# FFN1 of a gated-loop kernel wholly in three one-pass products, FFN2 plain, gates in two parts with five slots

## The chip, the cores and the metric

The kernel runs on one core of one Trainium2 chip. The metric is device time in microseconds (us). The profiler takes one execution apart: PE is TensorE (matmul), PEld its weight loads, DVE VectorE, ACT ScalarE, POOL GpSimd, SP SyncE, which here only issues DMAs.

## What is computed

A linear recurrence with complex decay per head (4 batches, 8 heads, 768 steps, head size 48), whose output goes as x (3072 x 384) into a feed-forward part:

```python
mag = np.sqrt(a_re * a_re + a_im * a_im)
scale = np.minimum(mag, 0.999) / (mag + 1e-06)       # a_n = a * scale
for t in range(S):
    S_re, S_im = ar*S_re - ai*S_im + outer(k[t], v[t]), ar*S_im + ai*S_re
    y[t] = q[t] @ S_re
x = y.transpose(0, 2, 1, 3).reshape(B * S, H * D)
out = (((x @ w1) * (x @ w2)) @ w3) @ w_out            # d_ff = 1024
```

Inputs are f32; the weights come as 64-bit floats and are rounded to f32 on the chip.

## The kernel before

**Units.** A unit is half a batch: 384 steps (TT) of all 8 heads, so there are eight (NU), in order. A unit has three stages.

- *Gates* (`gates`, passes over 128 x 1152 on ACT and DVE): logarithms and exponentials of the magnitude, arctangent, running product and running sum, sine and cosine, and from them q and k times cosine and sine (line 788 R = k*cos, 791 A = q*cos, 795 k*sin, 799 q*sin). Then DMAs ("move") lay them out by head in QL and KL. QL and KL exist once, so a unit's moves wait for the end of the unit before. The gates of u+1 begin with `gate_head` (Ln and Exp of re); the im rows of u+1 are loaded when lines 788 and 791 of u are done, as they take re's buffer.
- *Attention pieces* (`pieces`): transposes of R and k into KT ("tr"), states ("kv"), scores ("sc", with a masked copy on DVE), outputs ("y"). From unit 2 (THREE) on, "y" also makes three rounded forms of x: x0 on ACT, x1 on DVE, x2 on POOL.
- *FFN*: FFN1 makes a = x w1 and b = x w2 for eight blocks of 128 columns (j) and ab = a*b; FFN2 multiplies ab by w3o = w3 w_out (made once at the start), three tiles of 128 rows a unit.

**Products.** A plain product is three f32 matmuls (128 x 128 by 384 columns); the profile has two instructions for each. A *three-product* form splits weight and x into a coarse and a fine fp32r part, each multiplied in one pass: "hb" does coarse x coarse and fine x fine (six instructions), ACT rescales the PSUM bank in place (line 945), "db" adds the third product (three instructions) to the same bank, and DVE multiplies it into ab (line 929). Before, this holds for six of the 16 products of a unit, from unit 2 on: b for j < 6 (J3). The split weights are made once (`split_ops`: line 967 on ACT, 970 and 972 on DVE), in place of the whole ones, three of them (NB).

**FFN2** from unit 1 on takes tiles in pairs and multiplies 2 x 2 blocks with seven products instead of eight (`out_sums`, `out_pair`, line 1049: four matmuls of 192 columns each, sums on DVE). Every third tile is kept (`keep`) for a pair with the next unit's.

**Order.** The PE's order is a list: `unit(u, rest, ahead)` begins with AHEAD[u] items of the FFN of u-1, then mixes the rest of it with the pieces of u. The gates' steps, the splits and the checks are generators that yield (engine, cost, name, what it waits for); `run` walks the list, keeps a clock for each engine, and puts a step into its engine's queue where it `fits` before the next request of the list plus a slack (SLACK, LATE, EARLY). All engines run their queues in order. PSUM has four banks for the FFN (`ps_m`), two for tr, kv and y (`ps_v`).

**Memory.** A, R, q and k of a unit live in slots, six of them; the table SLOTS says which. The k and q rows of a unit are loaded in the middle of its gates, V rows (`load_v`) beside its predecessor's last state; the V tile with heads side by side (`turn_v`, 14 DMAs) is loaded after the predecessor's last y.

**Checks.** POOL looks through gates and weights for values that the fast path does not cover (`check_weights`); the last part of w3 is squared on POOL and tested on ACT (lines 1198, 1200). If one is found, a slow general kernel runs after all.

The lines that load k and q, that put the plain products ahead of the three-product ones, and that begin a unit's list:

```python
            if u > 2 and u not in LATER:      # gates(u), after the first logarithms
                load_qkv(u)
            ab = [[x for y in ab[J3:] for x in y] + [y.pop(1) for y in ab[:J3]]] + ab[:J3]   # ffn(u)
        seq = [("begin", u)] + rest[:ahead]   # unit(u)
```

Of the kernel before, what the change touches and what calls it, by code (L numbers as in the profile page):

```python
# [378 lines left out]
def kernel(  # L379
# [61 lines left out]
    J3 = NB * WB // P  # L441
    LATER = ()
# [29 lines left out]
    SLOTS = [dict(A=0, R=1, q=2, k=3), dict(A=4, R=5, q=0, k=2)]  # L472
# [69 lines left out]
    def take_qk(u):  # L542
        g = g_t.setdefault(u, {})
        g["q"] = slot(u, "q", "q")[:, :, 0:TT]
        g["k"] = slot(u, "k", "k")
# [7 lines left out]
    def load_qkv(u, key=None):  # L553
        b, h = divmod(u, 2)
        if "q" not in g_t.get(u, {}):
            take_qk(u)
        g = g_t[u]
        load_rows(g["k"], kt, u, key=key)
        load_rows(g["q"], qt, u)
        landed(("q", u), (), *(() if u in SPLIT else (2, 2.4)))  # L560
# [30 lines left out]
    def gate_head(u):  # L591

        g = g_t[u]
        g["A"], g["R"] = slot(u, "A", "gA")[:, :, 0:TT], slot(u, "R", "gR")
        yield "ACT", 2.45, "a1", (("re", u),)
        chain(nc.scalar.preload_act_table_set("natural_log_exp_and_others"))
        chain(nc.scalar.activation(out=g["A"], in_=g["re"], func=AF.Ln))
        yield "ACT", PASS, "r1", ("a1",)
        chain(nc.scalar.activation(out=g["R"][:, :, 0:TT], in_=g["A"], func=AF.Exp, scale=-1.0))

    def gates(u, split):
# [3 lines left out]
        if "A" not in g:  # L605
            g["A"], g["R"] = slot(u, "A", "gA")[:, :, 0:TT], slot(u, "R", "gR")
        A, R = g["A"], g["R"]
        Z = one.tile([P, KD, TT], FP, tag="gZ", name="gZ")
        re, im = g["re"], g["im"]
        r = R[:, :, 0:TT]  # L610
# [6 lines left out]

        if u < 2:
# [3 lines left out]
            for s in parts:  # L622
                act(out=A[:, s], in_=re[:, s], func=AF.Ln)
                yield "ACT", PASS, "r1", ("a1",)
                act(out=r[:, s], in_=A[:, s], func=AF.Exp, scale=-1.0)
# [7 lines left out]
        for i, s in enumerate(parts):  # L633
            yield "DVE", WIDE, "im", ("r1", ("im", u))
            tt(out=im[:, s], in0=im[:, s], in1=r[:, s], op=OP.mult)  # L635
# [11 lines left out]
        def operands():  # L647
            if u > 2 and u not in LATER:
                load_qkv(u)
            elif "q" not in g:  # L650
                take_qk(u)
            return g["q"], g["k"], g["k"][:, :, 0:TT]
        early = u > 1
        if early:
            q, K2, k = operands()
# [11 lines left out]
        for s in parts:  # L667
            yield "DVE", 1.0, "min", ("a2",)
            ts(out=A[:, s], in0=A[:, s], scalar1=0.999, scalar2=None, op0=OP.min)
            for f in range(s.start, s.stop):  # L670
                yield "DVE", SCAN, "mag", ("min", "z3")
                nc.vector.tensor_tensor_scan(out=A[:, f], data0=A[:, f], data1=Z[:, f], initial=1.0,  # L672
                                             op0=OP.mult, op1=OP.mult)
                if u > 1 and f < 2:
                    yield "ACT", 1.45, "low", ("im",)
                    check_gates(u, re, r, f)
        yield None

        for s in parts:
# [5 lines left out]
        if not early:  # L685
            q, K2, k = operands()

# [6 lines left out]
        def scaled(s):  # L694
            yield "DVE", WIDE, "k", ("r2", ("q", u))
            tt(out=k[:, s], in0=k[:, s], in1=r[:, s], op=OP.mult)
            if not early:
                yield "DVE", WIDE, "q", ("mag", ("q", u))
                tt(out=q[:, s], in0=q[:, s], in1=A[:, s], op=OP.mult)

        def ends():
            yield "ACT", 0.6, "ends", ("k",)
            for X in (R[:, :, TT], K2[:, :, TT], st_dec[:, u]):
# [5 lines left out]
        if u > 0:  # L709
            if early:  # L710
                yield "DVE", WIDE, "q", ("mag", ("q", u))
                tt(out=q, in0=q, in1=A, op=OP.mult)
# [23 lines left out]
        if u + 1 < NU:  # L736
            load_gates(u + 1, ("re",), ("ang",))
        yield None
# [23 lines left out]
        QL = one.tile([2 * D, H, TT], FP, tag="QL", name="QL")  # L762
        L_t[u] = QL, KL, R, K2
# [19 lines left out]
        if 0 < u < NU - 1:  # L783
            ops = gate_head(u + 1)
            g_t[u + 1]["head"] = [next(ops), ops]
            others.append(g_t[u + 1]["head"])
# [23 lines left out]
    def turn(u, c, x):  # L810
# [7 lines left out]
        with tc.high_priority():  # L818
            nc.scalar.copy(out=KT_t[u, c][:, :, :, x].rearrange("p h d f -> p f d h"),  # L819
                           in_=tp.rearrange("p f (d h) -> p f d h", h=H))  # L820

# [23 lines left out]
    def outputs(u, c):  # L845
# [3 lines left out]
        if c == 0:  # L849
            xT_t[u] = one.tile([P, KD, TT], FP, tag="xT", name="xT")  # L850
            if u >= THREE and NB:
# [15 lines left out]
        with tc.high_priority():  # L867
            if u in x_t:
                x = [t[:, :, w] for t in x_t[u]]
                nc.scalar.activation(out=x[0], in_=y, func=AF.Copy, scale=TOP / BITS)  # L870
# [5 lines left out]
            last["y", u, c] = nc.scalar.copy(out=xT_t[u][:, :, w], in_=y)  # L876
# [5 lines left out]
    def state(u, c):  # L882
# [19 lines left out]
        if 1 < u + 1 < NU and u + 1 not in LATER and c == UC - 1 - u % 2:  # L902
            load_v(u + 1)

    def ffn_ab(u, j):
# [32 lines left out]
        def heads():  # L938
            if u == THREE:
                while split_t[0] <= n and split_next():  # L940
                    pass
            got.append(bank())
            product(got[0], [(w3_h[n][:, :, w], x_t[u][0]), (w3_l[n][:, 0, :, w], x_t[u][1])])
            with tc.high_priority():
                nc.scalar.activation(out=got[0], in_=got[0], func=AF.Copy, scale=1.0 + 1.0 / BITS)  # L945

        def diffs():
            product(got[0], [(w3_l[n][:, 1, :, w], x_t[u][2])], False)
            times(got[0])

        if u >= THREE and j < J3:
            return [("hb", heads), ("ab1", first), ("db", diffs)]
# [8 lines left out]
    def split_ops():  # L961
        for n in range(NB):
            tag = f"w{n - 1}1" if n else "x0"
            yield "ACT", 0.85, ("head", n), (("tail", n - 1),) if n else ()
            pool = w12 if n else late[0]
            h = w3_h[n] = pool.tile([P, KD, WB], FR, tag=tag, name="wh", **({} if n else dict(padded_shape=[P, KD, TT])))
            nc.scalar.activation(out=h, in_=w_t[n][1], func=AF.Copy, scale=TOP * BITS)
            L = w3_l[n] = late[0].tile([P, 2, KD, WB], FR, tag=f"low{n}", name="low")
            yield "DVE", 1.0, ("tail", n), (("head", n),)
            nc.vector.scalar_tensor_tensor(out=L[:, 0], in0=w_t[n][1], scalar=BITS, in1=h, op0=OP.mult, op1=OP.subtract)  # L970
            yield "DVE", 1.0, ("diff", n), (("tail", n),)
            nc.vector.scalar_tensor_tensor(out=L[:, 1], in0=h, scalar=1.0 / BITS, in1=L[:, 0], op0=OP.mult, op1=OP.subtract)
            if n == NB - 1:
                yield "ACT", 0.85, ("head", 0), (("tail", n),)
                h = w12.tile([P, KD, WB], FR, tag=f"w{n}1", name="wh")
                nc.scalar.activation(out=h, in_=w3_h[0], func=AF.Copy)
                w3_h[0] = h
# [11 lines left out]
    KH, DH = KF // 2, DM // 2  # L989
    s_t = {}  # L990

    def out_weights():
        T = s_t["T"] = late[0].tile([P, 3, KH, DH], FP, tag="T", name="To")
        B = [[w3o[:, i * KH:(i + 1) * KH, j * DH:(j + 1) * DH] for j in range(2)] for i in range(2)]
        s_t["B"] = B[0][0], B[1][0], B[1][1], T[:, 2], T[:, 0], T[:, 1], B[0][1]
        for out, x, y in ((T[:, 0], B[0][1], B[0][0]), (T[:, 1], B[1][1], T[:, 0]), (T[:, 2], B[1][0], T[:, 1])):
            yield "DVE", 0.96, "out", ()
            nc.vector.tensor_tensor(out=out, in0=x, in1=y, op=OP.subtract)

    def last_weights():  # L1000
        B = s_t["B"]
        if len(B) == 7:
            nc.vector.tensor_tensor(out=B[6], in0=B[2], in1=B[6], op=OP.subtract)
            s_t["B"] = *B, None

    def keep(u):
        s_t["kept"] = late[0].tile([P, KF, P], FP, tag="kept", name="kept")
        nc.scalar.copy(out=s_t["kept"], in_=ab_t[u][:, :, 2 * P:3 * P])

    def out_sums(tiles):  # L1010
        S = s_t["S"] = late[0].tile([P, 3, KH, P], FP, tag="S", name="So")
        A = [[(s_t["kept"] if kept else ab_t[u][:, :, t * P:(t + 1) * P])[:, i * KH:(i + 1) * KH] for i in range(2)]
             for u, t, kept in tiles]
        s_t["sums"] = []
        with tc.high_priority():
            for i, (out, x, y, op) in enumerate(((S[:, 0], A[1][0], A[1][1], OP.add), (S[:, 1], S[:, 0], A[0][0], OP.subtract),
                                  (A[1][0], A[0][0], A[1][0], OP.subtract), (S[:, 2], A[0][1], S[:, 1], OP.subtract))):
                if i > 1:
                    s_t["sums"].append((out, x, y))
                else:  # L1020
                    nc.vector.tensor_tensor(out=out, in0=x, in1=y, op=op)
        s_t["A"] = A[0][0], A[0][1], S[:, 2], A[1][1], S[:, 0], S[:, 1], A[1][0]

    def out_pair(tiles):
        m, U, o = {}, {}, {}

        def add(out, x, y):
            nc.vector.tensor_tensor(out=out, in0=x, in1=y, op=OP.add)

        def done(t, half):  # L1030
# [712 lines left out]
```

## Time and profile before

| | |
|---|---|
| median of 3 runs | 540.72 us (537.26 to 541.58) |
| profiled execution | 539.31 us, span 537.5 us |
| PE busy | 505.5 us (94%) |
| DVE, ACT, POOL busy | 385.0, 314.9, 304.9 us |
| mean granted TensorE clock | 0.985 |

Busy time of an engine is the union of its instructions; matmuls overlap at their ends. "x552" counts instructions. A wait row names the instruction that waited, what released it, the total, the number of times and the longest. A row of the chain is start, length and what; its pieces follow one another without overlap. A row of windows is a stretch, its length, and busy time of each engine with the number of instructions, then the granted clock and the DMA share.

### The profile page before, as it was taken

How to read it: one execution, taken by the hardware profiler on the slowest of the kernel's cores; microseconds unless marked ns; L12 is line 12 of the kernel's file. 1: busy time of each engine (PE TensorE's matmuls, PEld its weight loads, DVE VectorE, ACT ScalarE, POOL GpSimd, SP SyncE). 2: the span in 40 equal slices, each digit the busy share in tenths (PEclk: the TensorE clock that was granted, in tenths of full speed). 3: DMA queues.
4: the chain of work that ended last, by engine and by line, in shares of the span. 5: the costliest groups of instructions: out<-in, count | busy, mean ns of one | idle time of the engine just before them, and what ended most of it. 6: DMA issues, size and time to landing. Idle time of an engine off the chain costs nothing.

```text
span 537.5 us, 13680 instructions
## 1 busy us (share of the span) xinstructions
PE 505.5 (94%) x5654; PEld 383.7 (71%) x5654; DVE 385.0 (72%) x581; ACT 314.9 (59%) x489; POOL 304.9 (57%) x343
## 2 busy tenths in 40 slices
PE   5689799998999999999998999999989999999994
PEld 2355575555756795888587985997679967995894
DVE  7999698867499888576857986688659882640171
ACT  6979866546566927646568426844777143258500
POOL 1000000028788989678967899669979898543000
PEclk9899899999999999999998999999999999999997
DMA  8999876694839736973598449955597247533001
GB/s 287 370 408 265 168 243 179 163 216 113 162 87 212 183 90 176 235 200 88 132 223 185 124 98 220 196 137 140 142 187 184 71 125 177 194 102 126 0 32 35
DMA packets 72456, 89.75 MB, mean 167 GB/s; under 512 B 30784, under 2 KB 62208, under 8 KB 71616
## 3 DMA queue, kind: packets, MB, share of 16 engines
q1 hardware_dynamic: 66464, 69.77, 51.5%
q0 software_dynamic: 5920, 19.01, 12.5%
q8 instruction: 46, 0.75, 0.6%
q14 instruction: 26, 0.21, 0.1%
HBM read 65.14 MB, written 4.72 MB: 130 GB/s over the span
## 4 chain that ended last, share of the span: by engine, by line
PE 67%; DVE 12%; ACT 8%; DMA 7%; issue 4%; SPq 1%; DVEq 0%; ACTq 0%
PE m L913 29%; PE p L1049 17%; PE y L866 7%; DMA im<-in_a_im_dram 5%; PE sc L831 5%; PE kv L891 2%; PE f L1339 2%; ACT gZ L614 2%; PE tp L817 2%; DVE gZ L732 2%; PE o L1087 1%; ACT KT L819 1%; ACT re L614 1%; DVE im L635 1%; DVE gA L672 1%
## 5 line engine op out<-in xcount | busy, mean ns | idle before, releaser
L913 PE MATMUL m<-xT,ws 128*128 128x384 f32 x552 | 180.0, 486 | 1.2 <-ACT xT L876 1.2
L913 PEld LDWEIGHTS m<-xT,ws 128*128 128x128 f32 x552 | 104.3, 190 | 71.9 <-ACT xT L876 1.7
L1227 POOL TENSOR_SCALAR look<-look 128x256 f32<-128x256 f32 (+1 forms) x64 | 77.9, 1218 | 5.6
L929 DVE TENSOR_TENSOR ab<-m,ab 128x384 f32<-128x384 f32 x64 | 35.1, 552 | 58.8 <-PE m L913 31.1
L925 ACT COPY ab<-m 128x384 f32<-128x384 f32 x64 | 30.1, 474 | 57.3 <-PE m L913 57.2
L1189 POOL TENSOR_TENSOR seen<-seen,look 128x256 bf16<-128x256 bf16 (+1 forms) x64 | 59.2, 925 | 5.2
L1173 POOL MEMSET seen<- 128x256 bf16 x1 | 0.3, 317 | 108.9 <-DVE ab L929 108.9
L913 PE MATMUL m<-x,low 128*128 128x384 f32 x216 | 47.8, 346 | 2.8 <-ACT m L945 2.7
L1224 POOL TENSOR_TENSOR look<-look 128x256 f32<-128x256 f32 (+1 forms) x52 | 38.7, 743 | 20.7 <-DMA look<-in_w_dram 12.9
L913 PEld LDWEIGHTS m<-x,low 128*128 128x128 f32 x216 | 37.9, 188 | 4.3 <-ACT m L945 4.2
L866 PE MATMUL y<-A,V 128*32 128x128 f32 x768 | 39.9, 272 | 0.4 <-issue 0.4
L870 ACT ACTIVATE x<-y 128x384 fp32r<-128x384 f32 x18 | 8.8, 491 | 51.8 <-PE y L866 51.8
L819 ACT COPY KT<-tp 128x384 f32<-128x384 f32 x40 | 34.7, 872 | 7.1 <-PE tp L817 6.9
L834 DVE COPY_PREDICATED A<-mask,sc 128x512 f32<-128x512 uint8 x48 | 32.6, 730 | 6.0 <-PE sc L831 6.0
L866 PE MATMUL y<-QL,T 96*32 96x128 f32 x640 | 35.5, 272 | 0.0
L866 PEld LDWEIGHTS y<-A,V 128*32 128x32 f32 x768 | 34.4, 110 | 0.9 <-issue 0.9
L1049 PE MATMUL p<-w3o,ab 128*128 128x192 f32 x192 | 35.0, 331 | 0.0
L831 PE MATMUL sc<-QL,KL 96*32 96x32 f32 (+3 forms) x1536 | 32.1, 235 | 1.5 <-DVE A L834 1.2
L1339 PE MATMUL f<-wo_s,w3s 128*128 128x384 f32 x96 | 33.4, 495 | 0.0
L1226 POOL TENSOR_SCALAR look<-look 128x192 f32<-128x192 f32 (+1 forms) x24 | 26.6, 1107 | 11.4 <-DMA look<-in_a_re_dram 10.0
L831 PEld LDWEIGHTS sc<-QL,KL 96*32 96x32 f32 x1536 | 28.4, 110 | 6.3 <-issue 3.4
L1049 PEld LDWEIGHTS p<-w3o,ab 128*128 128x128 f32 x192 | 31.8, 193 | 0.4 <-issue 0.2
(152 smaller groups left out, 1072.0 us busy)
## 6 DMA issues: line engine op xcount, KB each, us to landing
look<-in_w_dram POOLq DMA_DIRECT2D x36, 256.0 KB, 4.3
raw<-in_w_dram SPq DMA_DIRECT2D x6, 1024.0 KB, 9.9
looked<-in_w_dram POOLq DMA_DIRECT2D x10, 512.0 KB, 4.4
KL<-gR SPq DMA_DIRECT2D x24, 192.5 KB, 3.2
KL<-k SPq DMA_DIRECT2D x24, 192.5 KB, 6.9
vr<-in_v_dram SPq DMA_DIRECT2D x8, 576.0 KB, 6.4
QL<-gA SPq DMA_DIRECT2D x24, 192.0 KB, 7.4
QL<-q SPq DMA_DIRECT2D x24, 192.0 KB, 7.5
```

The costliest lines, as they stand in the source:

```text
L819: nc.scalar.copy(out=KT_t[u, c][:, :, :, x].rearrange("p h d f -> p f d h"), in_=tp.rearrange("p f (d h) -> p f d h", h=H))
L831: nc.tensor.matmul(out=sc[SB * g:SB * g + SB, j, s0:C], lhsT=KL[:, x * n + j, w][:, s0:s0 + SB], rhs=QL[:, x * n + j, w][:, s0:C], start=T ...
L834: last["sc", u, c, x] = nc.vector.copy_predicated(out=A[:, x * n:(x + 1) * n], data=sc, mask=mask)
L866: nc.tensor.matmul(out=o, lhsT=a, rhs=b, start=s0, stop=s1)
L913: nc.tensor.matmul(out=out, lhsT=a, rhs=b, start=start and i == 0, stop=i == len(terms) - 1, skip_group_check=not start)
L925: nc.scalar.copy(out=ab_t[u][:, j], in_=m)
L929: last["ab", u, j] = nc.vector.tensor_tensor(out=ab_t[u][:, j], in0=m, in1=ab_t[u][:, j], op=OP.mult)
L1049: nc.tensor.matmul(out=m[p], lhsT=a[:, f], rhs=b[:, f], start=(f == 0), stop=(f == KH - 1))
L1189: nc.gpsimd.tensor_tensor(out=seen[:, 0:n], in0=seen[:, 0:n], in1=x, op=OP.add)
L1224: tt(out=x, in0=x, in1=x, op=OP.mult)
L1227: ts(out=x, in0=x, scalar1=low, scalar2=None, op0=OP.is_ge)
L1339: nc.tensor.matmul(out=sums[j], lhsT=w3_t[f][:, j * P:(j + 1) * P], rhs=w3_t["wo"][:, f], start=(f == 0), stop=(f == KF - 1))
```

## The change

- **FFN1**: from unit 2 on every product, of w1 and of w2, is in three one-pass products. The tail of the w1 product ("da") is copied to ab by ACT, that of w2 ("db") multiplied by DVE. Heads run two ahead of tails (DEEP). Eight weight splits instead of three; all must be done before the first y of unit 2, since one uses x0's buffer for a time. x is no longer copied to xT from unit 2 on.
- **FFN2**: plain tiles; `out_weights`, `out_sums`, `out_pair`, `keep` go.
- **Gates** from unit 2 on (`gates_apart`): every pass in two parts, of 384 and 768 columns; five slots; the two range checks of re move into the head, ahead of its Ln; Exp of the head goes to re's buffer.
- **Loads**: k, q and V rows of u+1 are issued at the end of unit u, the first of them held behind the last y of u. For unit 2, k and q are issued at a transpose of unit 1.
- **Order**: `unit` shares the FFN out by planned PE time, not by count; AHEAD is in us. Slacks are wider. POOL's looks are held off 9 us before an x instead of 3. w3's late tests go from ACT to DVE. Two early weight loads are issued somewhat later.

```diff
-    AHEAD = [0, 3, 12, 15] + [8] * (NU - 4)
+    AHEAD = [0, 0, 23.0, 25.0] + [14.0] * (NU - 4)
-    PASS, WIDE, SCAN, LAND, SLACK, LATE, RING, NEAR, EARLY = 1.17, 1.48, 1.08, 1.8, 1.8, 2.4, 8, 4, 2
+    PASS, WIDE, SCAN, LAND, SLACK, LATE, RING, NEAR, EARLY = 1.17, 1.48, 1.08, 1.8, 2.6, 3.0, 8, 4, 2
-    THREE, NB = 2, 3
+    THREE, DEEP = 2, 2
-    HOLD, COSTS = 3.0, (4.9, 4.5, 6.8, 2.5)
+    HOLD, COSTS = 9.0, (4.9, 4.5, 6.8, 2.5)
-        SLOTS.append(dict(A=SLOTS[u - 2]["R"], R=SLOTS[u - 2]["k"], q=SLOTS[u - 1]["A"], k=SLOTS[u - 1]["q"]))
+        SLOTS.append(dict(A=SLOTS[u - 2]["k"], R=SLOTS[u - 1]["A"], q=SLOTS[u - 1]["q"], k=SLOTS[u - 1]["R"]))
+    def gates_apart(u, A, Z):
+        parts = [(0, slice(0, 1)), (1, slice(1, KD))]
...
+        for i, s in parts:
+            yield on("DVE", "im_", i, "r1", ("im", u))
+            tt(out=im[:, s], in0=im[:, s], in1=re[:, s], op=OP.mult)
...
+        for i, s in parts:
+            yield on("DVE", "kc_", i, ("cos_", i), ("k_", i))
+            tt(out=r[:, s], in0=k[:, s], in1=re[:, s], op=OP.mult)
+            move(KL, R, 0, i, s, "kc_")
...
+        if u + 1 < NU:
+            load_gates(u + 1, ("im",), (("kc_", 1), ("qc_", 1)))
...
+        def heads(m):
...
+            product(got[m], [(h[:, :, w], x_t[u][0]), (low[:, 0, :, w], x_t[u][1])])
+            with tc.high_priority():
+                nc.scalar.activation(out=got[m], in_=got[m], func=AF.Copy, scale=1.0 + 1.0 / BITS)
+        def diffs(m):
+            product(got[m], [(w3_l[n, m][:, 1, :, w], x_t[u][2])], False)
+            if m:
+                return times(got[1])
+            with tc.high_priority():
+                nc.scalar.copy(out=ab_t[u][:, j], in_=got[0])
+        if u >= THREE:
+            return [("hb", lambda: heads(0)), ("da", lambda: diffs(0)), ("hb", lambda: heads(1)), ("db", lambda: diffs(1))]
...
+    def ffn(u):
+        ab = [x for j in range(KF) for x in ffn_ab(u, j)]
+        if u >= THREE:
+            h, d = ab[0::2], ab[1::2]
+            ab = h[:DEEP] + [x for p in zip(h[DEEP:], d) for x in p] + d[-DEEP:]
+        return ab + [(("part", "half")[n], f) for t in range(UC) for n, f in enumerate(ffn_out(u, t, 2))]
...
             elif kind == "end":
...
+                if 0 < f < NU - 1:
+                    if f > 1:
+                        load_of(f + 1, "k", ("y", f))
+                        load_of(f + 1, "q")
                     load_v(f + 1)
```

More of the change, by code (lines that the diff above doesn't have):

```diff
@@ L593, in gate_head @@
         g = g_t[u]
-        g["A"], g["R"] = slot(u, "A", "gA")[:, :, 0:TT], slot(u, "R", "gR")
-        yield "ACT", 2.45, "a1", (("re", u),)
+        re = g["re"]
+        A = g["A"] = slot(u, "A", "gA")[:, :, 0:TT]
+        for f in range(2):
+            yield "ACT", 1.45, "low", (("re", u),)
+            check_gates(u, re, A, f)
+        if not g["go"]:
+            yield None
+        yield "ACT", 2.45, "a1", ("low",)
         chain(nc.scalar.preload_act_table_set("natural_log_exp_and_others"))
-        chain(nc.scalar.activation(out=g["A"], in_=g["re"], func=AF.Ln))
+        chain(nc.scalar.activation(out=A, in_=re, func=AF.Ln))
@@ L849, in outputs @@
         if c == 0:
-            xT_t[u] = one.tile([P, KD, TT], FP, tag="xT", name="xT")
-            if u >= THREE and NB:
+            if u < THREE:
+                xT_t[u] = (late[0].tile([P, KD, TT], FP, tag="x1", name="xT") if u else
+                           cv["early"].tile([P, KD, TT], FP, tag="xT", name="xT"))
+            else:
+                while u == THREE and split_next():
+                    pass
                 x_t[u] = [late[0].tile([P, KD, TT], FR, tag=f"x{i}", name=f"x{i}") for i in range(3)]
@@ L875, in outputs @@
                 later.append(rest)
-            last["y", u, c] = nc.scalar.copy(out=xT_t[u][:, :, w], in_=y)
+            else:
+                last["y", u] = nc.scalar.copy(out=xT_t[u][:, :, w], in_=y)
     Tb = [singles.tile([2 * D, H, 64], FP, name=f"T{i}") for i in range(3)]
@@ L961, in split_ops @@
     def split_ops():
[L962 to L977, printed above, removed]
+        which = [(n, m) for n in range(FF // WB) for m in (1, 0)]
@@ new lines, in split_ops @@
+        for i, (n, m) in enumerate(which):
+            yield "ACT", 0.85, ("head", i), (("tail", i - 1),) if i else ()
+            w = w_t[n][m]
+            if i:
+                h = w12.tile([P, KD, WB], FR, tag="w%d%d" % which[i - 1], name="wh")
+            else:
+                h = late[0].tile([P, KD, WB], FR, tag="x0", padded_shape=[P, KD, TT], name="wh")
+            w3_h[n, m] = h
+            nc.scalar.activation(out=h, in_=w, func=AF.Copy, scale=TOP * BITS)
+            L = w3_l[n, m] = late[0].tile([P, 2, KD, WB], FR, tag=f"low{n}{m}", name="low")
+            yield "DVE", 1.12, ("tail", i), (("head", i),)
+            nc.vector.scalar_tensor_tensor(out=L[:, 0], in0=w, scalar=BITS, in1=h, op0=OP.mult, op1=OP.subtract)
+            yield "DVE", 1.12, ("diff", i), (("tail", i),)
+            nc.vector.scalar_tensor_tensor(out=L[:, 1], in0=h, scalar=1.0 / BITS, in1=L[:, 0], op0=OP.mult, op1=OP.subtract)
+            if i == len(which) - 1:
+                yield "ACT", 0.85, ("head", 0), (("tail", i),)
+                h = w12.tile([P, KD, WB], FR, tag="w%d%d" % which[i], name="wh")
+                nc.scalar.activation(out=h, in_=w3_h[which[0]], func=AF.Copy)
+                w3_h[which[0]] = h
@@ L1000, in last_weights @@
[L1000 to L1022, printed above, removed]
@@ L1467, in start @@
     def start(op):
-        return max([clock[op[0]]] + [ready.get(x, 1e9 if type(x) is tuple and x[0] == 'q' else 0.0) for x in op[3]])
+        return max([clock[op[0]]] + [ready.get(x, 1e9 if type(x) is tuple and x[0] in ('q', 'k') else 0.0) for x in op[3]])
     def book(op):
```

413 lines of the change are left out of this document (228 added, 185 removed), and 5 rows, old and new, of the table TIMES.

## The prediction

> **What bounds the kernel now.** I read the page's head first, then the windows view cut at the ends of the units' last y, then the PE's waits.
>
> ```profile
> span 537.5 us, 13680 instructions
> ## 1 busy us (share of the span) xinstructions
> PE 505.5 (94%) x5654; PEld 383.7 (71%) x5654; DVE 385.0 (72%) x581; ACT 314.9 (59%) x489; POOL 304.9 (57%) x343
> ```
> ```profile
> sum 342.00, PE 336.45 PEld 267.64 DVE 254.40 ACT 193.39 POOL 276.72; mean PE 56.08 PEld 44.61 DVE 42.40 ACT 32.23 POOL 46.12
> ```
> ```profile
> PE m L913 <- ACT m L945: 2.7, 4, 0.8
> ```
>
> The sum row covers 140 to 482 us, six unit periods of 57 us on average: the PE is busy for 336.45 of 342 us. The other engines have room (DVE 254, ACT 193). So a microsecond less of matmul is a microsecond less of span, as long as nothing else becomes late; and all the PE ever waited for in FFN1 is 2.7 us, four times, for the scaling on ACT between the two halves of a three-product result (L945). There is little else to win: idle PE time in the middle is 5.5 us in all.
>
> **The change, part by part.** Rates come from the chain that ended last, where a piece starts when the one before ends, so pieces do not overlap.
>
> ```profile
> 166.34 1.94 PE m L913 x6
> ...
> 174.10 5.18 PE o L1087 x16
> ...
> 226.93 1.58 PE m L913 x9
> ...
> 511.25 6.50 PE p L1049 x40
> ...
> 517.88 11.91 PE p L1049 x72
> ```
>
> *FFN1.* A plain product (three f32 matmuls, two instructions each) takes 1.94 us, the same product as nine one-pass matmuls 1.58. In units 2 to 7 there are 16 products a unit, 96 in all; 36 are in three products already (six a unit). The change converts 60: 60 x 0.36 = **-21.6 us**.
>
> The Trainium skill, "TensorE: Matmul & The Clock Gate", section "Back-to-back issue gap", gives N/2.4 + 2.5 ns for a warm matmul, 162.5 ns for 384 columns; by it, as an estimate, nine would take 1.46 us, the term would be -28.8 and the time 526.5. The trace has 1.58 / 9 = 176 ns; it disagrees, the row decides, and the rule gets no chance of its own.
>
> *FFN2.* The seven-product form (56 instructions for two tiles) goes and plain tiles (16 instructions, 5.18 us) come back. The last two pairs took 6.50 + 11.91 = 18.4 us, 9.2 a pair, against 2 x 5.18 = 10.36 plain: +1.16 a pair. As a second look, busy time, which counts overlapping ends in both:
>
> ```profile
> 140.00:540.00 400.00, 97.92 (x560) 90.86 (x560) 0.99 0.58 140
> ```
>
> That is line L1049 alone: 97.92 us for 560 instructions, ten pairs, 9.8 each. Ten pairs cost between 10 x (10.36 - 9.8) = 5.6 and 11.6 us; I take **+11**, as the chain's rows measure like with like. So the two edits to the matmuls leave -10.6 us of PE work, half of what FFN1 alone would give.
>
> *What ACT and DVE get.*
>
> ```profile
> L945 ACT ACTIVATE m<-m 128x384 f32<-128x384 f32 x36 | 17.4, 485 | 14.7 <-PE m L913 13.6 <-DVE im L635 0.6
> ...
> L614 ACT ACTIVATE im<-im 128x1152 f32<-128x1152 f32 x7 | 8.2, 1165 | 0.1
> ...
> L614 ACT ACTIVATE im<-im 128x384 f32<-128x384 f32 x3 | 1.4, 513 | 0.0
> ```
>
> Per unit ACT gets ten more scalings (4.85 us); the copy of the first factor stays (now behind "da"). A gate pass in two parts costs 0.51 + 0.84 (from 384 columns at 0.513 and 1152 at 1.165, so 0.326 per 384 more) instead of 1.165; eleven passes, +2.0 us. Copies to xT and of the seven-product form go and plain tiles' copies come; I leave both out, since ACT's total is not the bound. So some 6 us a unit on top of 32: 38 of 55, still not the bound on average. DVE loses the sums and the seven-product adds and gains the splits. What counts is lateness. In a stream of three-product pieces two heads lie between a result's head and its tail (a head is six of the nine matmuls, 1.05 us, a tail three, 0.53; in the steady stream 2 x 1.05 + 2 x 0.53 us lie between), so ACT may be about 2.5 us late with the scaling; the four PSUM banks are live for some three of four periods, so the last evacuation may be about 1 us late. A plain product left two to three periods of 1.94. Behind a late ACT or DVE instruction stand these evacuations, and the PE behind them.
>
> The trace has this case: 36 such products cost 2.7 us of waits. 96 at the same rate cost 7.2: **+4.5 us**. Below, the waits could vanish altogether (-2.7), since smaller gate parts block for 0.84 instead of 1.165; above, every unit waits (second rival).
>
> *Eight weight splits instead of three*, between unit 1's FFN1 and unit 2's first y, where they are now forced:
>
> ```profile
> L970 DVE SCALAR_TENSOR_TENSOR low<-ws,wh 128x768 fp32r<-128x768 f32 x3 | 3.7, 1235 | 0.0
> ...
> L972 DVE SCALAR_TENSOR_TENSOR low<-wh,low 128x768 fp32r<-128x768 f32 x3 | 3.1, 1047 | 0.1
> ```
> ```profile
> 163.00:188.00 25.00, 24.79 (x322) 17.48 (x324) 22.04 (x27) 19.55 (x26) 21.86 (x20) 1.00 0.87 195
> ```
>
> One is 2.28 us of DVE: +11.4. In the stretch in which they must go DVE is busy for 22 of 25 us. With 22.04 - 3 x 2.28 + 8 x 2.28 = 33 it would be 8 us too much, less the sums that go: the splits fit only by pushing unit 3's gates back. Bounds 0 and +6; I take 0, because unit 3's transposes stand behind 25 us of FFN1 (AHEAD), longer than the push.
>
> *Loads of k, q, V rows at the unit's end, behind the last y.* What stands behind the waiting load on SP are the V loads, which wait for the same y now (the SP queue's own waits):
>
> ```profile
> SPq L577 <- PE y L866: 70.5, 13, 15.4
> ```
> ```profile
> k<-in_k_dram SPq DMA_DIRECT2D x7, 576.0 KB, 6.2
> q<-in_q_dram SPq DMA_DIRECT2D x7, 576.0 KB, 8.2
> ```
>
> So the wait itself costs nothing, but k and q now land some 7 and 9 us after the unit's end. Whether that is in time is read from unit 6, whose gates cross the end of unit 5's last y (where the chain's FFN2 pieces begin):
>
> ```profile
> 365.75 2.80 PE p L1049 x16
> ...
> 385.08 8.20 DMA im<-in_a_im_dram
> ```
> ```profile
> 381.12 1.82 DVE L788 TENSOR_TENSOR gR<-k,re 128x1152 f32<-128x1152 f32 x1 [2.56 <-ACT re L614]
> ...
> 393.37 1.36 DVE L635 TENSOR_TENSOR im<-im,gR 128x1152 f32<-128x1152 f32 x1 [1.92 <-ACT KT L819]
> ...
> 439.54 1.36 DVE L788 TENSOR_TENSOR gR<-k,re 128x1152 f32<-128x1152 f32 x1
> ```
> ```profile
> 388.78 0.49 PE L817 MATMUL tp<-ident,gR 128*128 128x128 f32 x3
> ```
>
> k times cosine (L788) starts 15 us after the end; k and q are there by then, so **0**. Bounds: 0, and 2 us a unit where a DVE instruction stands at its head waiting for k with evacuations behind it (+10), kept for the range. The transposes follow at 23 us; afterwards they come 14 us of FFN1 plus one or two FFN2 pieces after the end, 17 to 19 us. That is just behind L788's end at 382.9, and the cover of 6 us is gone.
>
> *Tests of w3 on DVE instead of ACT, the POOL held off 9 us before an x, the last tile out through ACT*: cover is the last FFN1, when DVE has no gates; I put +0.5 for the last copy and store, bounds 0 and 2.
>
> **Sum**, against the profiled execution (539.31 us, span 537.5): 539.3 - 21.6 + 11 + 4.5 + 0.5 = 533.7. The median of the three runs, 540.72, is 1.4 us higher; I name **533.5**.
>
> **The rivals.**
>
> *No new waits* (20%). Smaller parts let evacuations through. For it: parts of 0.51 and 0.84 us stand in an evacuation's way for less than the 1.165 of now, and DVE loses work. Against: ten more ACT instructions a unit. Then 539.3 - 10.6 = 528.7, and if some of the 5.5 us idle goes too, 524 to 529; I say 527.
>
> *Every unit's coupled stretch stalls and halves the clock* (24%). The waits come in two clusters, in units 4 and 6, and behind the first of them lies a half-clock window:
>
> ```profile
> 285.85 0.97 PE L913 MATMUL m<-x,low 128*128 128x384 f32 x3 [0.77 <-ACT m L945]
> ...
> 400.88 0.79 PE L913 MATMUL m<-x,low 128*128 128x384 f32 x3 [0.77 <-ACT m L945]
> ```
> ```profile
> 286.29:289.70 3.41, 3.41 (x57) 2.86 (x56) 2.77 (x5) 2.83 (x4) 2.91 (x5) 0.50 0.49 109
> ```
>
> It cost 3.41 / 2 = 1.7 us. If each of six units has one (+8.5) on top of the 4.5: 539.3 - 10.6 + 13 = 541.7, no change. The Trainium skill has this in "TensorE: Matmul & The Clock Gate", "A second HAM failure mode: psum-queue depth-cycling": micro-idles between groups that cycle through PSUM banks make the clock swing to half. The trace bears it out once in two clusters; in unit 6 the clock stayed full.
>
> *Slower: the loop of the gates becomes the bound* (14%). L788 of one unit releases the next im load, which takes 8.2 us, and from L635 to the next L788 it is 46 us (393.37 to 439.54): with the 12 us before (381.12 to 393.37) 58, hardly over the present period of 57. The PE's new period is about 57 - 10.6/6 = 55.2, so the loop must shrink by 3 us while ACT gets 6 us more a unit. If k's late arrival adds 3 us instead, the loop is 61 and five units pay 61 - 57.1 each: 539.3 + 19.5, less what units outside the loop save (two at 1.8): 555. It decides where L635 to L788 takes over 43 us. Against: much of those 46 us is low priority, not work; two parts overlap ACT and DVE.
>
> **How the numbers follow.** Forecast 38%, no new waits 20%, stalls and clock 24%, gate loop 14%, 4% for what I do not see (half of it slower). One per cent of 540.7, about what a measurement can tell from no change, is 5.4 us: faster is below 535.3. The forecast's own spread, 529 to 538, lies there with 31 of its 38 points; with the second case faster is 0.51, same 7 + 24 = 0.31, slower 0.18. The range goes from 524 (no waits at all) to 546 (the stalls with k's 2 us in half the units): above it most of the gate loop, 12%, below it 4%, and 4% unseen.
>
> **What would show it.** Right: L913's x9 pieces at 1.58 us, no p pieces, o pieces of 5.18; PE busy in the middle near 55 us a unit; PE m waiting for ACT m some 7 us; the clock at half once or twice. Wrong: PE tp waiting for ACT KT or DVE gR (gate loop); half-clock windows in most units; DVE k or q waiting for their DMA for several us with FFN evacuations behind; PE y or x waiting for DVE low at unit 2 (splits); POOL x late, so that the third products (x, low) wait for it.

## The result, and the profile after

The changed kernel took 555.83 us (median of 6 runs, 553.29 to 566.84) where the kernel before took 541.15 beside it: a ratio of 1.028 with an interval from 1.023 to 1.033. The forecast was 533.5, range 524 to 546. It is slower, by 14.7 us instead of 7 us faster.

The profiled execution took 555.77 us. The head of its page, to be held against the same lines of before:

```profile
span 553.9 us, 13674 instructions
## 1 busy us (share of the span) xinstructions
PE 505.6 (91%) x5594; PEld 384.8 (69%) x5594; DVE 373.5 (67%) x604; ACT 336.7 (61%) x569; POOL 244.2 (44%) x309
```

The PE is busy for as long as before (505.6 against 505.5), although FFN1 needs less of it, and the span is 16.4 us longer. So a part of the busy time ran slower, and idle time came. Where the idle time is, the PE's waits say (us in total, how often, the longest):

```profile
PE m L1058 <- ACT ab L1099: 11.1, 3, 5.4
...
PE sc L973 <- issue: 3.1, 1, 3.1
PE m L1058 <- ACT m L1092: 2.8, 2, 1.9
```

The first line is new: 11.1 us in only three waits of the FFN1 products. They are not the many small waits of 0.8 us for scalings that the prediction counted with (for those, L1092, the PE waited twice, 2.8 us in all). And the table by stage, cut at the ends of the last y of units 2 to 7, shows in which units the time went; its five stretches are units 3 to 7. First after, then before:

```profile
202.30:259.00 56.70, 54.39 (x685) 45.51 (x685) 42.71 (x58) 40.75 (x70) 34.55 (x40) 1.00 0.65 158
259.00:323.50 64.50, 58.08 (x707) 48.30 (x707) 38.41 (x55) 40.36 (x72) 32.42 (x40) 0.95 0.59 139
323.50:382.60 59.10, 54.40 (x677) 46.06 (x677) 37.82 (x54) 37.09 (x65) 33.16 (x44) 0.94 0.63 144
382.60:445.00 62.40, 59.54 (x716) 48.70 (x715) 41.16 (x59) 42.51 (x75) 34.45 (x46) 0.97 0.62 143
445.00:498.60 53.60, 51.74 (x678) 43.50 (x677) 24.66 (x35) 21.19 (x43) 30.15 (x36) 1.00 0.61 156
```
```profile
197.20:250.30 53.10, 51.35 (x667) 41.24 (x663) 38.52 (x50) 30.63 (x46) 42.66 (x48) 1.00 0.70 172
250.30:314.90 64.60, 62.96 (x745) 51.90 (x741) 50.19 (x66) 37.12 (x53) 53.41 (x56) 0.97 0.65 154
314.90:365.80 50.90, 50.90 (x663) 41.01 (x664) 37.13 (x48) 30.27 (x46) 39.27 (x49) 1.00 0.73 171
365.80:428.40 62.60, 61.22 (x741) 50.45 (x741) 50.36 (x66) 36.92 (x53) 55.38 (x59) 1.00 0.63 149
428.40:479.30 50.90, 50.90 (x665) 41.01 (x663) 27.77 (x39) 18.49 (x33) 36.87 (x42) 1.00 0.57 154
```

Behind the comma stands the stretch's length, then PE, PEld, DVE, ACT and POOL busy, the granted clock and the DMA share. (Before, two seven-product pairs fall in every second stretch and one in the others, so stretches are compared in twos.) After, the clock is 0.95, 0.94 and 0.97 in the stretches of units 4, 5 and 6, and the PE idles 6.4, 4.7 and 2.9 us in them. Units 3 and 7 have the full clock, with 2.3 and 1.9 us of idle time.

One of the three places, unit 4's coupled stretch, in four views. The SP queue from the end of unit 3's last y on:

```profile
260.00 0.61 SPq L527 DMA_DIRECT2D k<-in_k_dram  x1
260.78 0.60 SPq L527 DMA_DIRECT2D q<-in_q_dram  x1
261.47 0.56 SPq L561 DMA_DIRECT2D vr<-in_v_dram  x1
262.08 14.35 SPq L571 DMA_DIRECT2D V<-in_v_dram  x14
276.53 0.41 SPq L1159 DMA_DIRECT2D out_dram<-ot  x1
277.04 0.59 SPq L527 DMA_DIRECT2D re<-in_a_re_dram  x1
```

DVE's scans, whose last one frees the buffer into which that re goes:

```profile
263.03 3.68 DVE L666 TENSOR_TENSOR_SCAN gZ<-im 128x384 f32<-128x384 f32 x3
```

The scans ended at 266.7. The re load could go then, and goes at 277.04: for 10 us it stands behind the 14 loads of V rows. What ACT does meanwhile:

```profile
277.17 0.47 ACT L1092 ACTIVATE m<-m 128x384 f32<-128x384 f32 x1 [0.56 <-PE m L1058]
277.63 0.48 ACT L1099 COPY ab<-m 128x384 f32<-128x384 f32 x1
283.22 1.26 ACT L575 ACTIVATE gA<-re,consts 128x1152 f32<-128x1152 f32 x1 [5.10 <-DMA re<-in_a_re_dram]
...
284.47 0.47 ACT L1092 ACTIVATE m<-m 128x384 f32<-128x384 f32 x1
284.88 0.83 ACT L958 COPY KT<-tp 128x384 f32<-128x384 f32 x1
285.50 1.24 ACT L575 ACTIVATE gA<-re,consts 128x1152 f32<-128x1152 f32 x1
...
287.15 0.47 ACT L1099 COPY ab<-m 128x384 f32<-128x384 f32 x1
```

The range check of the next unit's re (L575) is at the head of ACT's queue and waits for the load; behind it in the queue stand the scaling of a product (L1092), a copy of transposes (L958) and a copy of the first factor (L1099), none of which needs re. The banks stay full, and the PE:

```profile
287.67 1.33 PE L1058 MATMUL m<-x,wh 128*128 128x384 f32 x3 [5.38 <-ACT ab L1099]
```

It names the copy it waited for, not the load two steps back. Units 5 and 6 have the same (ACT waits of 5.97 and 3.68 us at L575). Behind each lies a stretch at half clock (columns as above, the clock is 0.50):

```profile
286.37:293.20 6.83, 5.53 (x17) 5.53 (x18) 0.56 (x1) 5.11 (x9) 2.98 (x5) 0.50 1.09 239
347.81:354.64 6.83, 5.73 (x18) 5.30 (x19) 1.15 (x2) 5.14 (x11) 2.57 (x5) 0.50 1.08 227
409.25:412.66 3.41, 3.41 (x13) 3.31 (x12) 0.00 (x0) 2.08 (x4) 2.43 (x5) 0.50 1.09 210
```

The PE was busy for 5.53 + 5.73 + 3.41 = 14.67 us there at half speed, so some 7 us of its work was lost to the clock, besides the idle time.

Before, re stood behind V too, but it came in time: in unit 5's stretch V took 8.14 us, re went at 322.59 us, its first reader, Ln in the next unit's head, came at 328.48 without a wait, and the checks from 348.42 on.

```profile
313.37 8.14 SPq L577 DMA_DIRECT2D V<-in_v_dram  x14
...
322.59 0.59 SPq L529 DMA_DIRECT2D re<-in_a_re_dram  x1
```
```profile
328.48 1.18 ACT L597 ACTIVATE gA<-re 128x1152 f32<-128x1152 f32 x1
```

So the load came later; its reader did not come earlier. Counted from the last y of the unit before, re was issued after 7.7 to 9.9 us in units 3 to 6 before, and after 16.2 to 18.0 us in units 4 to 6 of the changed kernel, where it was there after 22.2 to 24.2. ACT came to its first reader after 13.6 to 18.8 us before (Ln), and after 17.3 to 19.1 us in the changed kernel (the check): no earlier.

### The profile page after: what moved, and what is told of

Read it like the earlier page. It is cut to its first block, busy times and chain, and to the rows that moved or that the text cites. A ratio compares the mean times of both kernels' runs of the same rounds, so it can differ in the third digit from the quotient of the medians.

```text
span 553.9 us, 13674 instructions
## 1 busy us (share of the span) xinstructions
PE 505.6 (91%) x5594; PEld 384.8 (69%) x5594; DVE 373.5 (67%) x604; ACT 336.7 (61%) x569; POOL 244.2 (44%) x309
## 4 chain that ended last, share of the span: by engine, by line
PE 67%; DVE 11%; DMA 8%; ACT 7%; issue 5%; SPq 1%; ACTq 0%; DVEq 0%
PE m L1058 28%; PE o L1153 20%; PE y L1012 7%; PE sc L973 5%; DMA re<-in_a_re_dram 3%; PE kv L1038 2%; PE f L1415 2%; PE tp L956 2%; DMA QL<-q 1%; DMA KL<-k 1%; DVE low L1124 1%; ACT KT L958 1%; DMA im<-in_a_im_dram 1%; ACT re L616 1%; DMA k<-in_k_dram 1%
## 5 line engine op out<-in xcount | busy, mean ns | idle before, releaser
L1153 PE MATMUL o<-w3o,ab 128*128 128x384 f32 x384 | 132.7, 495 | 0.0
L1058 PE MATMUL m<-x,low 128*128 128x384 f32 x576 | 123.0, 347 | 2.8 <-ACT m L1092 2.8
L1058 PEld LDWEIGHTS m<-x,low 128*128 128x128 f32 x576 | 106.5, 194 | 3.4 <-issue 2.1
L1153 PEld LDWEIGHTS o<-w3o,ab 128*128 128x128 f32 x384 | 71.0, 191 | 46.2 <-issue 3.5
L1058 PE MATMUL m<-x,wh 128*128 128x384 f32 x288 | 72.2, 360 | 11.5 <-ACT ab L1099 11.1
L1092 ACT ACTIVATE m<-m 128x384 f32<-128x384 f32 x96 | 45.3, 475 | 33.5 <-PE m L1058 32.2
L1058 PE MATMUL m<-xT,ws 128*128 128x384 f32 x192 | 63.1, 487 | 1.1 <-ACT xT L1023 1.1
L1058 PEld LDWEIGHTS m<-x,wh 128*128 128x128 f32 x288 | 52.6, 195 | 15.5 <-ACT ab L1099 12.6
L1020 POOL TENSOR_TENSOR x<-x,x 128x384 fp32r<-128x384 f32 x18 | 23.1, 1284 | 72.2 <-DVE x L1019 72.2
L1058 PEld LDWEIGHTS m<-xT,ws 128*128 128x128 f32 x192 | 36.0, 190 | 25.5 <-ACT xT L1023 1.7
L958 ACT COPY KT<-tp 128x384 f32<-128x384 f32 x40 | 33.9, 863 | 4.9 <-PE tp L956 4.5
```

Of the source, the lines that this page charges most:

```text
L1020: nc.gpsimd.tensor_tensor(out=x[2], in0=x[1], in1=x[0], op=OP.subtract)
L1058: nc.tensor.matmul(out=out, lhsT=a, rhs=b, start=start and i == 0, stop=i == len(terms) - 1, skip_group_check=not start)
L1092: nc.scalar.activation(out=got[m], in_=got[m], func=AF.Copy, scale=1.0 + 1.0 / BITS)
L1153: nc.tensor.matmul(out=m, lhsT=ab_t[u][:, f, t * P:(t + 1) * P], rhs=w3o[:, f], start=(f == 0), stop=(f == KF - 1))
```

## The experiments

The theory (1): ACT's checks wait for a re that V's loads hold back, evacuations stand behind them, the clock halves after the gap. The rivals: (2) the loop of the gates is too long, as the prediction's slower case has it (its 555 is the time that came); (3) more DMA traffic delays the PE's instructions (its stops named "issue").

**The re load out of V's way, on POOL's queue.** In the loads of re from unit 3 on:

```
-            load_rows(g[n], src, u)
+            load_rows(g[n], src, u, None, nc.gpsimd if n == "re" and u > 2 else None)
```

> Edit: in the changed kernel only the queue of one load is another: re of units 3 to 7 is issued by POOL, at the same place of the program, so that it goes as soon as DVE's last scan has ended; the 14 V loads and the moves stay where they are on SP. Theory 1: re lands 8 to 10 us earlier, the waits of 5.10, 5.97 and 3.68 us at ACT's checks go, and the scores' wait for QL (3.9 us with re ahead of V on SP) doesn't come: 535 to 541 us. Theory 2 (gate loop): 553 or more. If POOL, which waits in order for the scan, delays the third operand of the products, PE m waits for POOL x.

Measured: 542.12 us (12 runs) beside 542.97 before, ratio 0.996 (0.992 to 1.0005), a little above the 535 to 541 that theory 1 gave. In its trace V takes 14.21 us on SP in unit 4 as it did, re no longer stands behind it, and two waits are left at ACT's checks: 2.8 us for unit 2's re, which stayed on SP, and 0.8 in unit 4 (its row names V):

```profile
276.22 0.79 POOL L527 DMA_DIRECT2D re<-in_a_re_dram  x1
```
```profile
281.84 1.26 ACT L575 ACTIVATE gA<-re,consts 128x1152 f32<-128x1152 f32 x1 [0.83 <-DMA V<-in_v_dram]
```

In unit 4 POOL issued re 6.6 us after the scans' end (it had tests of its own to do first), so re went only some 4 us earlier than in the changed kernel, not 8 to 10; in units 5 and 6 it was 8 us, counted from the last y. That was enough. Its stages, to be laid beside the two tables above:

```profile
205.20:261.90 56.70, 54.71 (x687) 45.52 (x685) 41.52 (x58) 40.62 (x70) 36.02 (x41) 1.00 0.65 158
261.90:319.30 57.40, 55.30 (x707) 45.70 (x708) 39.05 (x55) 40.19 (x72) 34.28 (x40) 1.00 0.67 156
319.30:371.90 52.60, 52.03 (x677) 43.68 (x677) 39.17 (x55) 37.10 (x65) 37.22 (x45) 1.00 0.70 162
371.90:429.60 57.70, 57.21 (x715) 47.18 (x715) 41.18 (x59) 42.26 (x75) 37.30 (x47) 1.00 0.66 154
429.60:483.20 53.60, 51.80 (x681) 43.56 (x677) 24.63 (x35) 21.17 (x43) 30.46 (x36) 1.00 0.61 156
```

The three damaged stretches are 7.1, 6.5 and 4.7 us shorter, 18.3 in all, and the clock is 1.00 in each: the gap and the half clock go together. The first and the last stretch are the same to the tenth. This shows theory 1. ACT's instructions stand in the same order as in the changed kernel, and nothing in the loop of the gates was edited. Theory 2 has its own sign in the prediction: im times re to k times cosine (L635 to L788) over 43 us. In the changed kernel these are L625 and L717, and from start to start it took 37.7, 40.0 and 38.6 us in units 4, 5 and 6 (45 to 48 before); in unit 5:

```profile
301.02 0.56 DVE L625 TENSOR_TENSOR im<-im,re 128x384 f32<-128x384 f32 x1 [0.43 <-ACT re L599]
...
341.06 0.55 DVE L717 TENSOR_TENSOR gR<-k,re 128x384 f32<-128x384 f32 x1
```

This part of the loop was shorter, not longer, in the very units that lost the time. What became longer is the rest, from L717 to the next L625, which has the wait for re in it: 24.4, 19.9 and 19.9 us, against 17.7, 13.4 and 15.3 with re on POOL. So theory 2, as the prediction has it, is out.

**The re load ahead of V, both on SP.** The 14 V loads are put off until the re load is issued.

```
-                    turn_v(f + 1)
+                    held_v.append(rows)         # at the unit's end
...
             load_gates(u + 1, ("re",), (("ang_", 1),))
+            while held_v:
+                held_v.pop()()
```

> Edit: the 14 V loads of the next unit, which stand ahead of the re load in SP's queue (262.08 to 276.43 us in the changed kernel's trace, while DVE's last scan before the re load ended at 266.7), are issued right behind that re load instead. Theory 1 (ACT's range checks of re wait for a late re, hold the evacuations behind them, and the half clock follows): re lands about 9 us earlier, the waits of 5.10, 5.97 and 3.68 us at L575 go, the PE's gaps of 5.38 and 4.48 us and most of the half clock behind them go: 536 to 544 us. Theory 2 (the gate loop is longer than the PE's work): nothing is gained, 553 or more, as the moves come behind V. Theory 3 (DMA traffic slows the PE's instruction fetch): 551 to 555.

Measured: 541.46 us, ratio 1.002 (0.991 to 1.012). No wait for re is left, and the price is a new one, as the moves now stand behind V:

```profile
PE sc L975 <- DMA QL<-q: 3.9, 2, 3.0
```

Two different edits with the same effect on re give the same 14 us back; here, too, ACT's order is that of the changed kernel.

**The checks left out.** The two passes of L575 are gone, Ln of re is now the first reader.

> Edit: the two range checks of re are left out from unit 2 on (12 ACT passes of 1.26 us; the part of the validity test that they feed then counts them as passed). Ln of re stands at the head in their place and reads the same re. Theory 1: what hurts is the wait for re, not the passes; Ln waits in the checks' place about as long, so two thirds or more of the loss stays: 548 to 555 us. Rival (ACT has too much work around the coupled stretch, and the checks are the two passes too many): the waits go, 537 to 543.

Measured: 572.47 us, ratio to before 1.055 (1.042 to 1.069): outside both expectations. The part that it was to show is in the trace: Ln waits in the checks' place, three times, 15.9 us in all (14.8 in the changed kernel); the first of them:

```profile
284.21 1.16 ACT L594 ACTIVATE gA<-re 128x1152 f32<-128x1152 f32 x1 [5.14 <-DMA re<-in_a_re_dram]
```

So the wait is tied to re, not to the checks or their own 2.5 us. But with twelve passes fewer the planner wrote another order, in which the PE waits 12.7 us for scalings (L1089) and 6.6 us for products on DVE; the 17 us beyond the changed kernel were not taken apart further. An edit that also moves the order written out is a poor test of one wait; the two above leave the order of ACT alone.

**The planner's price of V.**

```
-                    landed("V", (), 14, 0.3, 0.57)
+                    landed("V", (), 14, 0.3, 1.03)
```

> Edit: one number of the planner: a V load is priced at 1.03 us of SP (14.35 us for 14 in the changed kernel's trace) instead of 0.57, so that the order written out for ACT and DVE expects re later. No instruction is added or taken away; checks and Ln of re stand some 6 us later in ACT's order. Theory 1: ACT no longer waits for re with evacuations behind, 538 to 546 us. Theory 2 (gate loop): the head of the gates comes later still, slower than 556, up to 575.

Measured: 560.61 us, ratio 1.038 (1.028 to 1.048). A miss of the experiment: the checks stayed at nearly the same place in ACT's order, and ACT waited 14.8 us for re as in the changed kernel (three waits of up to 5.6). So it tells nothing on theory 2 either, though the time lies in the range that theory 2 gave.

**k and q of unit 2 later.** Twice: at unit 1's end, and behind its second scores (with V on POOL).

> Edit: k and q of unit 2 are loaded at unit 1's end (about 146 us) as those of the later units, instead of behind unit 1's second transposes (124.05 and 124.83 us). Theory 3 (the loads raise the DMA share to 0.98 while the PE's 16 KB instruction fetch is under way, and the PE stands 3.10 us in the middle of the scores with a half-clock window behind): that stall and the window at 132.8 us go, 3 to 6 us less, 550 to 553 us. Rival (the stall is tied to the place in the program, not to the transfers): the stall stays and the time stays at 555 to 557. Theory 1 says nothing else changes: the waits for re at 283, 347 and 405 us stay.

> Edit: as the kernel with V on POOL, and besides k and q of unit 2 are loaded behind unit 1's second scores (about 133 us) instead of behind its second transposes (about 124 us). Theory 3 (those loads delay the PE's instruction fetch and cost a stop of 3 us in unit 1's scores with a half-clock window behind): another 3 to 5 us less than the kernel with V on POOL alone, 531 to 536 us. Rival (the stop comes at this place of the program anyway): same as that kernel within 2 us.

Measured: 563.51 us (ratio 1.040, 1.026 to 1.054) and 567.44 (1.050, 1.043 to 1.058; the kernel that it is compared with, 569.47). The stop in unit 1's scores was absent in the first one's profile (y had one of 3.1 us instead) and 3.4 us long in the second's; in the profile of the kernel with V on POOL, where k and q were loaded early, it was 0.6. So it is not bound to those loads; theory 3 found no support. The first is 8 us slower than the changed kernel, and its trace shows theory 1's wait in one more unit. With k and q ahead of them, V's loads at unit 1's end took 11.52 us instead of 8.29, re went 14.2 us after the last y instead of 5.5, and ACT waited for it a fourth time:

```profile
167.62 1.25 ACT L575 ACTIVATE gA<-re,consts 128x1152 f32<-128x1152 f32 x1 [7.04 <-DMA re<-in_a_re_dram]
```

From unit 1's last y to unit 2's it is 64.6 us in its profile, 56.5 in the changed kernel's: 8.1 us more.

**V last, and V on POOL.** Three tries for a version without the new wait for QL.

> Edit: as in the kernel with the re load ahead of V, but the 14 V loads go behind the unit's last move (QL from q) instead of right behind the re load. In that kernel (541.5 us) the moves stood behind V and the scores waited 3.9 us for QL. Theory 1: those 3.9 us go, re is still early, 536 to 540 us, unless V becomes late for its first y: then PE y waits for the V load by up to 5 us in each odd unit, 541 to 548. Theory 2 (gate loop): as before, 541.

> Edit: as in the kernel with the re load ahead of V, but the 14 V loads of a unit are issued by POOL at that place instead of by SP, so that nothing on SP stands behind them. Theory 1: no wait for re at ACT's checks, no wait of the scores for QL: 535 to 539 us. If POOL's issuing holds up the third operand of the products (x from POOL), PE m waits for POOL x and it is 541 or more.

> Edit: V on POOL behind the re load as in the run of 569.5 us, but the planner counts nothing for POOL's 14 issues, so POOL's tests of w3 are written out as early as in the changed kernel. In that run the middle was at the level of the kernel before up to unit 6 (428.6 us against 428.4 at its last y), and 19.9 us were lost at the end, where the count waited for tests that were late. Theory 1: without this tail 538 to 543 us. If POOL's tests come late all the same (9 us of issuing a unit are real), 550 or more.

Measured: 547.42 (ratio 1.012, 1.004 to 1.019), 569.47 (1.058, 1.053 to 1.063) and 547.11 us (1.010, 1.006 to 1.014). Behind the moves V brings no gain: the scores' wait is 5.9 us, put down to V. On POOL V pushes back POOL's tests of w3, and the loss comes at the end:

```profile
PE count L1445 <- DVE tot L1440: 19.9, 1, 19.9
...
PE m L1060 <- POOL x L1022: 5.5, 1, 5.5
```

With nothing counted for V in the plan (the third) the tail is gone, but POOL's third operand is late once, for 7.4 us, and the time lies between the two expectations. One load moved to POOL is cheap; fourteen, 8.9 us of issuing a unit, are not.

**FFN2 plain alone, in the kernel before.**

```
-        if u == 0:
-            return ab + [(("part", "half")[n], f) for t in range(UC) for n, f in enumerate(ffn_out(u, t, parts))]
+        return ab + [(("part", "half")[n], f) for t in range(UC) for n, f in enumerate(ffn_out(u, t, 2))]
```

> Edit: the kernel before with its FFN2 plain from unit 1 on (no seven-product pairs, no sums and differences for them), nothing else changed. The prediction's term for this edit was +11 us (bounds 5.6 and 11.6): 552 us beside 541 for the kernel before. If the seven-product form's additions on DVE also hold up evacuations, plain gives some of it back and it is 546 to 549; if the whole loss of the change came from here it would be 555 or more.

> Edit: the kernel before with plain FFN2 (561.7 us) and two of the planner's bounds as in the changed kernel (SLACK 2.6 for 1.8, LATE 3.0 for 2.4), no instruction added or taken away. FFN2's own matmuls took 10.1 us more in that run's trace than before, the rest of its +21.8 stood elsewhere. If the rest comes from where the planner puts ACT's and DVE's gate work between the evacuations, it changes by several us either way, 550 to 558 or over 565; if it belongs to plain FFN2 itself, 560 to 563.

Measured: 561.69 us (ratio 1.036, 1.029 to 1.044) and 561.45 (1.033, 1.025 to 1.041), more than any bound of the term, and in the range expected if the whole loss of the change came from here. FFN2's own matmuls are as forecast: 384 of them are busy for 130.42 us, against 97.92 (quoted in the prediction) and 21.84 for the two lines of before, so +10.7.

```profile
0.00:600.00 600.00, 130.42 (x384) 71.01 (x384) 0.98 0.58 150
```
```profile
0.00:600.00 600.00, 21.84 (x64) 11.76 (x64) 0.99 0.58 150
```

The other 8 to 11 us are in part waits of the PE for scalings (8.3 us against 2.7 before); the planner's two bounds don't change them (8.8), and what makes them stays open. It is not the loss of the change: with re on POOL FFN2 is just as plain, and units 3 to 7 together are 4.1 us shorter than before (278.0 against 282.1).

**Once more the same kernels,** for the scatter of the first units.

> The kernel before, unchanged, for a second profile. If the early loss belongs to the change: unit 2's last y ends within 2 us of the first profile's 197.2 us, half-clock windows before it add up to 7 us, PE stops at issue to under 1 us. If it comes and goes: the end of unit 2 scatters by 5 us or more, with half-clock windows of 10 to 17 us.

> The kernel before, unchanged, for a third profile; expected as for the second.

> The kernel with re on POOL's queue, unchanged, for a second profile. If the early loss belongs to the change: unit 2's last y ends at 203 to 206 us again, and the stretch from there to unit 6's last y takes 224 to 225 us again (231.2 before). If it comes and goes: the end of unit 2 moves by 5 us or more, and the later stretch stays.

Measured: 542.38, 543.79 and 540.55 us. Unit 2's last y of the kernel before ended at 197.2, 199.1 and 205.9 us in its three profiles; with re on POOL at 205.2 and 204.1. The third profile of before has the stops that the first had not:

```profile
PE y L866 <- issue: 4.6, 2, 2.4
```

So a difference as large as that of the first units comes and goes without any change. Behind unit 2's last y the three profiles of before take 340.3, 341.5 and 336.1 us, the two with re on POOL 333.4 and 334.7; if the change with re on POOL gains anything, it is there, 1 to 8 us. And the profile on which the sum was made was a short one (539.31 against 542.38 and 543.79).

## Why the prediction was wrong, by its steps

*What bounds the kernel: right.* Where nothing was late, less PE work was a shorter span: units 3 to 7 took 282.1 us before (the five stretches), 278.0 with re on POOL.

*FFN1, -21.6: nearly right.* All of FFN1's matmuls with re on POOL, then before:

```profile
0.00:538.00 538.00, 224.67 (x1056) 187.71 (x1056) 0.98 0.65 167
```
```profile
0.00:537.00 537.00, 243.31 (x876) 160.22 (x876) 0.99 0.65 167
```

That is -18.6 of busy time. In the changed kernel the chain has 25.46 us for 16 products, 1.59 each, where 1.58 was forecast:

```profile
506.58 25.46 PE m L1058 x144
532.04 10.32 PE o L1153 x32
```

The Trainium skill's formula that was set aside ("TensorE: Matmul & The Clock Gate", section "Back-to-back issue gap", given there for an isolated matmul) has, as an estimate, 1.46; the row disagrees.

*FFN2, +11: nearly right.* The same chain has 10.32 us for two tiles (10.36 forecast). By busy time the term is +10.7 alone and, with re on POOL, +13.1 (132.87 against 119.76):

```profile
0.00:538.00 538.00, 132.87 (x384) 71.07 (x384) 0.98 0.65 167
```

The matmuls together are -5.5 where -10.6 was forecast.

*Small waits for ACT, +4.5: too large.* FFN1's waits for scalings and copies are 3.2 us with re on POOL, against 2.7 before and 7.2 forecast: +0.5. 96 products did not wait at the rate of 36.

*Splits, 0: nothing against it;* no wait of the PE names them. *The loop of the gates: not what came,* as it was 38 to 40 us where it had to be over 43, though its 555 is the measured time; that is luck, and a rival that hits the number can still be the wrong one.

*Loads at the unit's end, 0, and bounds 0 and +10: the step that failed.* It asked what stands behind the held loads on SP and answered with the V loads alone, then followed k to a reader. Behind V stood re, which the same lines push back: in unit 4 to 18 us after the last y (8 in unit 5 before), as k, q and vr go first and V takes 14.35 us instead of 8.14. ACT came to re's first reader after 17 to 19 us, much as before, and waited 14.8 us in three units; with re out of V's way the three stretches are 18.3 us shorter. The prediction followed no reader of re. It also saw, in this step, only DVE as the engine on which a waiting instruction would hold evacuations; it was ACT. That the checks had moved to the head did not make the wait: without them Ln waited for the same re.

The reader to which k was followed, L788, was not its first one either: k times the magnitude (L681 in the changed kernel) comes 6 to 8 us after the last y, and DVE waited there for k once, 3.2 us, in unit 7. The term 0 for k held, but with no cover.

*The clock:* the second rival's mechanism, half clock behind waits, came with another cause and in three units, not six. The Trainium skill, "TensorE: Matmul & The Clock Gate", section "HAM oscillation — how this bites in real kernels", has the rule that PE gaps above some 3.4 us bring the clock down; gaps of 5.38 and 4.48 us, with 6.83 us at half clock that begin 1.3 and 1.1 us before their ends, agree. In unit 6, 3.41 us followed single gaps of no more than 1.22, which that rule does not cover.

*What is left:* with re on POOL 542.1 remains against 533.5. Five us are in the matmuls (-5.5 for -10.6). Some 4 are in the base, a short profile: it was 539.3, and the kernel before took 543.0 beside this run. The prediction had read that the median was 1.4 us above its base and yet named 533.5, where its sum, moved by that, gives 535.1. The small waits give 4 us back, and the rest, some 4, is not settled; the first three units end at 204 to 205 us in both profiles with re on POOL, at 197 to 206 in those of before. No version here beats the kernel before by more than can be measured.

## What to carry to other kernels

Where a load is moved, list every later load on the same queue, and follow each to its first reader, not only the one that the edit is about. At that reader, ask when the engine comes to it, when its data lands, and which instructions stand behind it in the engine's queue that need nothing of it. Gaps cost more than their length when the clock falls behind them (in the three stretches 10.8 us more idle time became 18.3). A load with another queue (one issue on POOL) was worth 14 us here, more than both edits to the matmuls brought together.

## What the runs showed of the hardware that was not expected

Issuing the same 14 V loads took 8.1 to 9.1 us on SP before, 12.3 to 14.4 in the changed kernel where k, q and vr were issued just ahead (8.3 at unit 1's end, where only vr was), 8.9 to 12.4 right behind re, and 8.9 on POOL where nothing interrupted it: an issue had no fixed price, and what sets it was not tested. The PE stopped at issue for 0.6, 3.2 and 5.3 us in all in three profiles of the kernel before, nearly always among the short matmuls of scores and y; no edit here removed it for sure.
